# Gathers of the unit two ahead spread over the first product, all seven row splits beside the last three tiles of the second

## The chip, the cores and the metric

The kernel runs on one core of one Trainium2 chip. The metric is the device time of one execution in microseconds (us). TensorE (PE) multiplies, VectorE (DVE) and ScalarE (ACT) do the elementwise work, GpSimd (POOL) does some of it and issues the indirect DMAs (gathers and scatters by row number), SyncE (SP) issues plain DMAs and DMA transposes. Each engine, and each engine's queue of DMA issues, works strictly in the order of the program; engines wait for each other by semaphores.

## The reference

A block-sparse attention is followed by a top-2 mixture of experts. The part that matters here is the second:

```python
def _moe_ref(x, w_gate, w_noise, noise, w1, w2) -> np.ndarray:
    N, D = x.shape                      # 3072, 512
    E = w_gate.shape[1]                 # 8 experts, w1[e] 512x1024, w2[e] 1024x512
    ...
    top2 = np.argpartition(-noisy_logits, 2, axis=1)[:, :2]
    ...
    for e in range(E):
        for k in range(2):
            mask = top2[:, k] == e
            ...
            h = np.maximum(x[mask] @ w1[e], 0.0)
            out[mask] += top2_w[mask, k, None] * (h @ w2[e])
    return out.astype(np.float32)
```

## The kernel before, in words

The first half of the run is attention and routing and is not touched. The second half works through nine units, numbered u = 0 to 8: u = 0 and u = 1 share expert 0, and u = 2 to 8 are the experts 1 to 7 with 816 rows each, six chunks of 128 rows and one of 48. Every unit gathers its rows, splits them into a high and a low float16 half, turns them, multiplies by w1 (the first product), applies the rectifier, multiplies by w2 (the second product) and adds its weighted rows to the output by an indirect DMA.

From u = 3 on (`BLOCKS = 3`) the first product, `mm1_blocks`, uses seven block products in the place of eight. It runs in four sets i = 0 to 3. A set is seven products of six matmuls into PSUM banks named `ph`; ACT copies the first two banks to SBUF (lines L1026 and L1029, tile `area`), DVE adds and subtracts banks and copies (L1022), and `hidden` (L999 on ACT, L1000 on DVE) makes the high and low halves `hh`, `hl`. The fourth product of a set adds to the first bank, so PE cannot begin it until ACT has copied that bank. In the middle of each set one quarter of w2 is split: two ACT operations (L851, L852) and one subtraction on POOL (L853, tile `w2l`).

The second product, `mm2`, takes seven tiles k = 0 to 6, one for each chunk of rows, and each tile ends in `finish`: ACT scales the bank into one of three buffers `y` (L1104) and POOL scatters it with an add (L1109). Before tile k, `make_next(u + 1, k)` prepares the next unit: the splits of its w1 blocks (L880, L881), the sums of its row blocks and their splits into `tx` (L889 to L902), and the loads of its raw weights `wraw` on SP (L834), which rotate through six buffers. `row_split(1)`, the last of these splits, is needed by the fifth product of the next unit's first set.

Rows are fetched two units ahead. `meta` and `indices` are two small DVE operations (L909, L915), `gather` one indirect DMA on POOL for each chunk (L929) into the only row buffer `xg`; so a chunk can be gathered for the next unit only after the chunk of that number has been split. A split is one ACT copy (L948) and one DVE subtraction (L949) into one of five buffers `xs`, and one DMA transpose on SP (L953) turns it into `xt`, of which there are two, one for even and one for odd units. `xg`, `xs` and some other tiles lie in one large tile that the profile calls `kv`.

In the kernel before, this fetch is cut into pieces, by hand: chunks 0 to 3 of unit u + 2 are gathered before the last tile of unit u - 1, chunks 4 to 6 at sets 0 to 2 of unit u; chunks 0 to 2 are split ahead of set 0 of unit u (`halves`) and turned at tile 0; chunk 3 is split and turned at tile 0, and chunks 4, 5 and 6 at tiles 3, 4 and 5.

Of the kernel before, what the change touches and what calls it, by code (L numbers as in the profile page):

```python
# [747 lines left out]
class Experts:  # L748
# [188 lines left out]
                    self.tc.declare_no_dep(g.ins, s.ins, reason="other rows")  # L937
            ro.early.append(g)

    def row_halves(self, u, c):  # L940
        r = self.st["u", u]
        if "xt" not in r:
            pool, x = (self.xta, "a") if u % 2 == 0 else (self.xtb, "b")
            r["xt"] = pool.tile([P, self.KB, 2, 7 * P], F16, name="xt" + x)
        x = self.xg[:, c].rearrange("p (k c) -> p k c", c=P)
        xs = r["xs", c] = self.xs[0]
        self.xs = self.xs[1:] + self.xs[:1]
        self.nc.scalar.activation(xs[:, :, 0], x, AF.Copy)  # L948
        self.nc.vector.tensor_tensor(xs[:, :, 1], x, xs[:, :, 0], op=ALU.subtract)  # L949

    def turn_halves(self, u, c):
        r = self.st["u", u]
        self.nc.sync.dma_start_transpose(out=r["xt"][:, :, :, c * P:(c + 1) * P].rearrange("p k a r -> p (k a) r"),  # L953
                                         in_=r.pop(("xs", c)).rearrange("p k a c -> p (k a c)"))

    def xpose(self, u, c):
        self.row_halves(u, c)
        self.turn_halves(u, c)

    def chunks(self, u):  # L960

# [251 lines left out]
def kernel(ctx, tc, q, k, v, v_windows, sampled_blocks, w_gate, w_noise, noise, w1, w2, out):  # L1213
# [11 lines left out]
    ex = Experts(tc, router, w1, w2, out, x_dram, table)  # L1225
# [136 lines left out]
    nu = len(ex.units)  # L1362
# [31 lines left out]
            rest = third()  # L1394
            next(rest)

    def gathers(u, chunks):
        for i in chunks:
            ex.gather(u, i)

    def halves(u, chunks):
        for i in chunks:
            ex.row_halves(u, i)

    def fetch(u, chunks=None):
        ex.meta(u)
        ex.indices(u)
        gathers(u, range(ex.count(u)) if chunks is None else chunks)

    def make_next(u, k):  # L1410
        e = ex.units[u][1]
        if k == 0:
            if u + 1 < nu:
                for c in range(3):
                    ex.turn_halves(u + 1, c)
            for n in range(0 if u == BLOCKS else 2, 4):
                ex.weight_sum(e, 0, n)
            ex.weight_split(e, 0, 0)
            ex.load_piece(e, 4)
        elif k == 1:  # L1420
            ex.weight_split(e, 0, 1)
            ex.load_piece(e, 5)
        elif k == 2:
            ex.weight_split(e, 0, 2)
            ex.row_parts(u)
            ex.load_piece(e, 6)
        elif k == 3:
            ex.row_sums()
        elif k == 4:
            for n in range(4):  # L1430
                ex.weight_sum(e, 1, n)
            ex.weight_split(e, 1, 0)
        elif k == 5:
            ex.weight_split(e, 1, 1)
            ex.row_split(0)
            ex.load_piece(e, 7)
        else:
            ex.weight_split(e, 1, 2)
            ex.row_split(1)
        if u + 1 < nu and k in (0, 3, 4, 5):  # L1440
            ex.xpose(u + 1, {0: 3, 3: 4, 4: 5, 5: 6}[k])
        if u + 2 < nu and k == 6:
            fetch(u + 2, range(4))

    for u in range(nu):
        if u == 2:
# [5 lines left out]
        n = full + bool(left_)  # L1452
        nx = 1 < u < nu - 1
        if u >= BLOCKS:
# [5 lines left out]
            for i in range(ex.FB // 2):  # L1460
                if u + 2 < nu:
                    if i == 0:
                        halves(u + 2, range(3))
                    gathers(u + 2, ((4,), (5,), (6,), ())[i])
                ex.mm1_blocks(u, i, early)
                if nx:
                    for j in ((0, 1, 2), (3,), (), ())[i]:
# [1 line left out]
        else:  # L1469
            for f in range(ex.FB):  # L1470
# [13 lines left out]
                if u == 2:  # L1484
# [9 lines left out]
                            ex.load_piece(e + 1, i)  # L1494
                    if f == 5:
                        fetch(4)
                    if f == 7:
                        halves(4, range(3))
        for k, c in enumerate(ex.chunks(u)):
            if nx:  # L1500
                make_next(u + 1, k)
# [72 lines left out]
```

## Time and profile before

| what | us |
|---|---|
| median of three runs | 872.43 |
| lowest and highest of the three | 862.88, 872.71 |
| the profiled execution | 867.12 |
| its span | 865.1 |

The span is the time from the first to the last instruction on the core; the 2.0 us between it and the time of the profiled execution lie around it. All times in the rows below are counted from the start of the span. Units u = 3 to 8 begin their first products at 447.26, 518.17, 589.20, 660.50, 730.37 and 793.38 us.

### The profile page before, as it was taken

To read this page: it belongs to the slowest core of one execution; us is meant where nothing else is said; L and a number is where in the kernel's file an instruction comes from. 1 tells how busy PE (TensorE), PEld (TensorE's weight loads), DVE (VectorE), ACT (ScalarE), POOL (GpSimd) and SP (SyncE) were. 2 spreads that over 40 slices of the span, in tenths; PEclk is the share of its full clock that TensorE was granted. 3 is DMA by queue.
4 is the path that set the end of the run, shared out by engine and by line. 5 is a ranking of instruction groups with operands and counts; after the bars stand their busy time and mean duration, and the time that the engine had idled before them with its cause. 6 is when DMAs were issued, how large, how long until landed. Compare 5 with 4: busy or idle time off the path is not lost.

```text
span 865.1 us, 20964 instructions
## 1 busy us (share of the span) xinstructions
PE 778.4 (90%) x8505; PEld 461.6 (53%) x8505; DVE 551.7 (64%) x1086; ACT 417.6 (48%) x730; POOL 335.8 (39%) x525
## 2 busy tenths in 40 slices
PE   3899869988987799999988997997997999999995
PEld 1567657766666676565434443543543544544542
DVE  4676568767596566516776784784785686785620
ACT  2575544545662533525446554644645546635610
POOL 2566555622374200614544225235324332333232
PEclk9999898999997999999998998998999999999998
DMA  9988996881596985959993675367179267343013
GB/s 326 318 248 258 287 271 221 287 269 52 168 264 165 207 291 185 213 156 169 302 196 105 124 129 149 82 136 203 37 153 196 84 137 155 85 98 50 1 27 52
DMA packets 136249, 148.22 MB, mean 171 GB/s; under 512 B 65988, under 2 KB 101828, under 8 KB 136144
## 3 DMA queue, kind: packets, MB, share of 16 engines
q1 hardware_dynamic: 97200, 75.76, 32.0%
q0 software_dynamic: 16720, 45.77, 22.7%
q10 hardware_dynamic: 22224, 25.27, 10.1%
q8 instruction: 69, 1.13, 0.5%
q14 instruction: 36, 0.29, 0.1%
HBM read 105.87 MB, written 27.10 MB: 154 GB/s over the span
## 4 chain that ended last, share of the span: by engine, by line
PE 20%; issue 17%; DMA 9%; POOL 5%; ACT 2%; DVE 1%; POOLq 0%; ACTq 0%
PE ph L1018 13%; PE py L1062 7%; DMA out_dram<-y,mt 7%; POOL out_dram L1109 2%; DMA kv<-x_rows,gi 2%; POOL kv L929 1%; POOL w2l L853 1%; DVE area L1022 1%; ACT hh L999 1%; PE py L1073 1%; ACT w2h L852 0%; ACT wraw L851 0%; ACT area L1026 0%; ACT area L1029 0%; POOLq L1109 0%
## 5 line engine op out<-in xcount | busy, mean ns | idle before, releaser
L1109 POOL DMA_INDIRECT out_dram<-y,mt x56 | 86.6, 1546 | 243.2 <-ACT y L1104 188.9
L1062 PE MATMUL py<-w2h,hh 128*128 128x512 f16 x384 | 145.6, 379 | 0.0
L1062 PE MATMUL py<-w2h,hl 128*128 128x512 f16 x384 | 145.5, 379 | 0.0
L1062 PE MATMUL py<-w2l,hh 128*128 128x512 f16 x384 | 145.5, 379 | 0.0
L1062 PEld LDWEIGHTS <-hh 128*128 128x128 f16 x768 | 74.6, 98 | 90.1 <-issue 2.5
L317 ACT ACTIVATE t<-t 128x512 f32<-128x512 f32 (+1 forms) x120 | 63.1, 567 | 99.3 <-PE t L315 98.6
L1018 PEld LDWEIGHTS <-w1a 128*128 128x128 f16 x672 | 67.5, 100 | 77.7 <-issue 29.7
L1104 ACT ACTIVATE y<-py,r_tab 128x512 f32<-128x512 f32 (+1 forms) x55 | 37.7, 685 | 137.8 <-PE py L1062 90.8
L1018 PE MATMUL ph<-tx,w1a 128*128 128x408 f16 x384 | 101.5, 347 | 0.0
L214 POOL COPY kg<-kv 128x128 f32 x264 | 70.3, 311 | 51.0 <-issue 17.6
L853 POOL TENSOR_TENSOR w2l<-wraw,w2h 128x1024 f16<-128x1024 f32 x24 | 51.6, 2149 | 96.5 <-ACT w2h L852 96.5
L303 ACT ACTIVATE p<-s,nm 128x256 f32<-128x256 f32 x176 | 69.5, 480 | 25.6 <-DVE nm L264 24.0
L929 POOL DMA_INDIRECT kv<-x_rows,gi x56 | 60.9, 1088 | 46.5 <-DVE gi L915 23.9
L315 PE MATMUL t<-ident,p 128*128 128x128 f32 x448 | 70.5, 299 | 4.5 <-ACT p L303 2.2
L1000 DVE SCALAR_TENSOR_TENSOR hl<-ph,hh 128x408 f16<-128x408 f32 (+2 forms) x64 | 32.5, 531 | 59.9 <-ACT hh L999 59.9
L315 PEld LDWEIGHTS t<-ident,p 128*128 128x128 f32 x448 | 51.3, 149 | 36.4 <-issue 17.9
L1022 DVE TENSOR_TENSOR area<-ph,area 128x408 f32<-128x408 f32 x96 | 53.5, 578 | 21.5 <-PE ph L1018 14.3
L999 ACT ACTIVATE hh<-area 128x408 f16<-128x408 f32 (+1 forms) x48 | 33.0, 713 | 70.8 <-DVE area L1022 70.8
L1018 PE MATMUL ph<-tx,w1b 128*128 128x408 f16 x192 | 66.2, 345 | 0.0
L243 PE MATMUL s<-kg,q 64*32 64x256 f32 x1408 | 56.5, 404 | 9.2 <-issue 4.8
L949 DVE TENSOR_TENSOR kv<-kv 128x512 f16<-128x512 f32 x56 | 38.3, 689 | 40.9 <-ACT kv L948 40.8
L264 DVE TENSOR_REDUCE nm<-s 128x4 f32<-128x1024 f32 (+1 forms) x48 | 54.2, 1129 | 14.2 <-PE s L243 13.2
(202 smaller groups left out, 1439.6 us busy)
## 6 DMA issues: line engine op xcount, KB each, us to landing
wraw<-in_moe_w_dram SPq DMA_DIRECT2D x64, 512.0 KB, 5.6
vb<-in_v_windows_dram ACTq DMA_DIRECT2D x24, 390.0 KB, 5.5
vb<-in_v_windows_dram ACTq DMA_DIRECT2D x16, 520.0 KB, 6.1
kv<-in_v_dram SPq DMA_DIRECT2D x4, 1560.0 KB, 15.6
q<-in_q_dram SPq DMA_DIRECT2D x12, 512.0 KB, 6.3
kv<-in_k_dram SPq DMA_DIRECT2D x8, 768.0 KB, 9.5
out_dram<-zero ACTq DMA_DIRECT2D x8, 768.0 KB, 4.8
x_rows<-xr SPq DMA_DIRECT2D x19, 256.0 KB, 3.9
```

What stands on the lines that cost most here:

```text
L214: nc.gpsimd.tensor_copy(KG[:, j, :, 32 * s:32 * s + 32], KT[:, :, bass.ds(offs[3 * j + s], 32)])
L243: mm = lambda out, l, r, pos: nc.tensor.matmul(out, l, r, start=True, stop=True, tile_position=pos)
L264: red = lambda out, x: nc.vector.tensor_reduce(out, x, axis=AX.X, op=ALU.max, negate=True)
L303: self.nc.scalar.activation(p[:, 256 * u:256 * u + 256], S[:, a, 256 * r:256 * r + 256], AF.Exp, bias=nb[:, u:u + 1], scale=1.0 if k else ...
L315: self.nc.tensor.transpose(T[i][:, c:c + P], p[:, i * w + c:i * w + c + P], self.ident)
L317: self.nc.scalar.activation(t[:, i * w:(i + 1) * w], T[i][:, 0:w], AF.Copy)
L853: self.nc.gpsimd.tensor_tensor(lo, t, hi, op=ALU.subtract)
L929: g = nc.gpsimd.indirect_dma_start(out=self.xg[0:m, c], out_offset=None, in_=self.x_dram[0:nr], in_offset=bass.IndirectOffsetOnAxis(ap=r[" ...
L1018: nc.tensor.matmul(bank[:, 0:HC], self.wop[part][:, w, kb, fs], b(kb, a), start=start and n == 0, stop=n == 5, skip_group_check=True)
L1022: add = lambda e, out, p, q: e.tensor_tensor(out, p, q, op=ALU.add)
L1062: nc.tensor.matmul(py, h[:, f, o], w[x][:, f, :], start=i == 0, stop=i == last)
L1109: s = nc.gpsimd.indirect_dma_start(out=self.out, out_offset=bass.IndirectOffsetOnAxis(ap=r["mt"][0:m, c:c + 1], axis=0), in_=y[0:m], in_of ...
```

## The change

The gathers of unit u + 2 now all stand in the first product of unit u, two ahead of each of the sets 0, 1 and 2 and one ahead of set 3, with `meta` and `indices` ahead of set 0. All seven splits, each with its transpose, stand in the second product of unit u: two before tile 4, two before tile 5, three before tile 6, each time behind the work on the next unit's weights and row sums. Nothing is added or taken out; `row_halves` and `turn_halves` become one function again.

```diff
-    def row_halves(self, u, c):
+    def xpose(self, u, c):
...
-        xs = r["xs", c] = self.xs[0]
+        xs = self.xs[0]
         self.xs = self.xs[1:] + self.xs[:1]
         self.nc.scalar.activation(xs[:, :, 0], x, AF.Copy)
         self.nc.vector.tensor_tensor(xs[:, :, 1], x, xs[:, :, 0], op=ALU.subtract)
-
-    def turn_halves(self, u, c):
-        r = self.st["u", u]
         self.nc.sync.dma_start_transpose(out=r["xt"][:, :, :, c * P:(c + 1) * P].rearrange("p k a r -> p (k a) r"),
...
     def make_next(u, k):
         e = ex.units[u][1]
         if k == 0:
-            if u + 1 < nu:
-                for c in range(3):
-                    ex.turn_halves(u + 1, c)
...
-        if u + 1 < nu and k in (0, 3, 4, 5):
-            ex.xpose(u + 1, {0: 3, 3: 4, 4: 5, 5: 6}[k])
-        if u + 2 < nu and k == 6:
-            fetch(u + 2, range(4))
+        if u + 1 < nu and k > 3:
+            for c in range(ex.count(u + 1))[2 * k - 8:2 * k - 6 if k < 6 else None]:
+                ex.xpose(u + 1, c)
...
             for i in range(ex.FB // 2):
                 if u + 2 < nu:
                     if i == 0:
-                        halves(u + 2, range(3))
-                    gathers(u + 2, ((4,), (5,), (6,), ())[i])
+                        ex.meta(u + 2)
+                        ex.indices(u + 2)
+                    for c in range(2 * i, min(2 * i + 2, n)):
+                        ex.gather(u + 2, c)
                 ex.mm1_blocks(u, i, early)
...
                     if f == 5:
                         fetch(4)
-                    if f == 7:
-                        halves(4, range(3))
```

How the order of instructions moves is shown at two engines, at the border between two units (the same at the borders ahead of u = 3, 4, 5 and 6). First ACT, before: the last two tiles of a unit's second product, then set 0 of the next unit. L880 and L901 are the next unit's splits, L1104 the tile's scaling into `y`, L948 the row splits, L1026 the copy of the first bank.

```order
L1104 ACTIVATE y<-py,r_tab 128x512
L880 ACTIVATE w1a<-wraw 128x4x256
L901 ACTIVATE tx<-area 128x4x408
L948 ACTIVATE kv_89<-kv_89 128x4x128
L1104 ACTIVATE y<-py,r_tab 128x512
L880 ACTIVATE w1a<-area 128x6x256
L901 ACTIVATE tx<-area 128x4x408
L1104 ACTIVATE y<-py,r_tab 128x512
L948 ACTIVATE kv_89<-kv_89 128x4x128 x3
L1026 ACTIVATE area<-ph 128x408
```

The same place of ACT in the changed kernel (its lines have other numbers: L1097 is the scaling into `y`, L1019 the copy of the first bank):

```order
L1097 ACTIVATE y<-py,r_tab 128x512
L880 ACTIVATE w1a<-wraw 128x4x256
L901 ACTIVATE tx<-area 128x4x408
L948 ACTIVATE kv_89<-kv_89 128x4x128 x2
L1097 ACTIVATE y<-py,r_tab 128x512
L880 ACTIVATE w1a<-area 128x6x256
L901 ACTIVATE tx<-area 128x4x408
L948 ACTIVATE kv_89<-kv_89 128x4x128 x3
L1097 ACTIVATE y<-py,r_tab 128x512
L1019 ACTIVATE area<-ph 128x408
```

The three splits have moved from behind the last tile's scaling to ahead of it, and they are now those of chunks 4 to 6, gathered a product earlier. Next POOL, before, from the scatters of one unit's second product to its next:

```order
L1109 DMA out_dram<-y,mt 3072x512 x6
L929 DMA kv_89<-x_rows,gi 128x512 x4
L1109 DMA out_dram<-y,mt 3072x512
L929 DMA kv_89<-x_rows,gi 128x512
L853 TENSOR_TENSOR w2l<-wraw,w2h 128x1024
L929 DMA kv_89<-x_rows,gi 128x512
L853 TENSOR_TENSOR w2l<-wraw,w2h 128x1024
L929 DMA kv_89<-x_rows,gi 48x512
L853 TENSOR_TENSOR w2l<-wraw,w2h 128x1024 x2
```

The same place of POOL in the changed kernel (L1102 is the scatter):

```order
L1102 DMA out_dram<-y,mt 3072x512 x7
L929 DMA kv_89<-x_rows,gi 128x512 x2
L853 TENSOR_TENSOR w2l<-wraw,w2h 128x1024
L929 DMA kv_89<-x_rows,gi 128x512 x2
L853 TENSOR_TENSOR w2l<-wraw,w2h 128x1024
L929 DMA kv_89<-x_rows,gi 128x512 x2
L853 TENSOR_TENSOR w2l<-wraw,w2h 128x1024
L929 DMA kv_89<-x_rows,gi 48x512
L853 TENSOR_TENSOR w2l<-wraw,w2h 128x1024
```

The four gathers that stood ahead of the seventh scatter now stand behind it, and the first `w2l` of the unit has two gathers ahead of it and the seventh scatter ahead of those.

## Rows read from the trace of the kernel before

**Rows 1.** Waits of PE from 440 us on: us in total, times, longest.

```profile
PE ph L1018 <- ACT area L1026: 22.3, 4, 6.0
```

**Rows 2.** Timeline of PE (start, us, what): first matmuls of units 3, 5, 7, 8.

```profile
447.26 0.51 PE L1018 MATMUL ph<-xtb,w1a 128*128 128x408 f16 x2
...
589.20 0.51 PE L1018 MATMUL ph<-xtb,w1a 128*128 128x408 f16 x2
...
730.37 0.51 PE L1018 MATMUL ph<-xtb,w1a 128*128 128x408 f16 x2
...
793.38 0.51 PE L1018 MATMUL ph<-xta,w1a 128*128 128x408 f16 x2
```

**Rows 3.** Timeline of PE in set 0 of unit 5; brackets: idle before, releaser.

```profile
592.13 0.34 PE L1018 MATMUL ph<-tx,w1b 128*128 128x408 f16 x1
597.85 0.84 PE L1018 MATMUL ph<-xtb,w1a 128*128 128x408 f16 x2 [5.39 <-ACT area L1026]
...
603.85 0.34 PE L1018 MATMUL ph<-xtb,w1a 128*128 128x408 f16 x1
```

**Rows 4.** Stretches: busy us and instructions by engine, granted clock, DMA share, GB/s.

```profile
598.00:603.00 5.00, 5.00 (x16) 2.22 (x15) 1.29 (x3) 2.60 (x4) 3.51 (x3) 0.50 0.48 93
...
731.00:760.00 29.00, 29.00 (x169) 16.31 (x167) 18.52 (x32) 17.49 (x27) 10.10 (x5) 1.00 0.37 97
```

**Rows 5.** Timeline of ACT at the border from unit 4 to 5.

```profile
586.22 1.55 ACT L901 ACTIVATE tx<-area 128x1632 f16<-128x1632 f32 x1
589.45 0.69 ACT L1104 ACTIVATE y<-py,r_tab 128x512 f32<-128x512 f32 x1 [1.67 <-issue]
594.62 0.63 ACT L948 ACTIVATE kv<-kv 128x512 f16<-128x512 f32 x1 [4.49 <-DMA kv<-x_rows,gi]
...
597.31 0.49 ACT L1026 ACTIVATE area<-ph 128x408 f32<-128x408 f32 x1
```

**Rows 6.** Timeline of POOL at the same border.

```profile
590.44 1.07 POOL L929 DMA_INDIRECT kv<-x_rows,gi  x1 [3.66 <-DVE gi L915]
...
595.77 1.70 POOL L1109 DMA_INDIRECT out_dram<-y,mt  x1 [0.30 <-issue]
```

**Rows 7.** Timeline of DVE from tile 4 of unit 4 to that border.

```profile
579.17 0.68 DVE L949 TENSOR_TENSOR kv<-kv 128x512 f16<-128x512 f32 x1
...
588.03 1.85 DVE L902 TENSOR_TENSOR tx<-area,tx 128x1632 f16<-128x1632 f32 x1
...
590.00 0.17 DVE L915 TENSOR_SCALAR gi<-mt 128x7 int32<-128x7 int32 x1
595.28 0.69 DVE L949 TENSOR_TENSOR kv<-kv 128x512 f16<-128x512 f32 x1 [5.11 <-ACT kv L948]
```

**Rows 8.** Stretch of tiles 4 to 6 of unit 4; columns: PE, PEld, DVE, ACT, POOL.

```profile
573.70:589.20 15.50, 15.50 (x74) 6.98 (x73) 12.62 (x14) 9.27 (x10) 4.68 (x3) 1.00 0.73 134
```

**Rows 9.** DMA from issue to landing: transposes to xta, 440 to 735 us.

```profile
DMA to landing us min/median/max: 3.1/4.1/6.2
```

**Rows 10.** The same of the raw weights' loads, 440 to 800 us.

```profile
DMA to landing us min/median/max: 3.3/5.7/8.7
```

**Rows 11.** Timeline of POOL at the border from unit 6 to 7.

```profile
726.40 1.55 POOL L1109 DMA_INDIRECT out_dram<-y,mt  x1 [3.68 <-ACT y L1104]
735.33 1.55 POOL L1109 DMA_INDIRECT out_dram<-y,mt  x1 [7.38 <-ACT w2h L852]
736.34 2.71 POOL L853 TENSOR_TENSOR w2l<-wraw,w2h 128x1024 f16<-128x1024 f32 x1
743.32 2.13 POOL L853 TENSOR_TENSOR w2l<-wraw,w2h 128x1024 f16<-128x1024 f32 x1 [4.27 <-ACT w2h L852]
```

**Rows 12.** Timeline of DVE in sets 0 and 2 of unit 7.

```profile
738.39 1.11 DVE L1022 TENSOR_TENSOR area<-area 128x408 f32<-128x408 f32 x1
...
748.22 0.68 DVE L863 TENSOR_TENSOR area<-wraw 128x512 f32<-128x512 f32 x1
748.82 0.57 DVE L1022 TENSOR_TENSOR area<-ph,area 128x408 f32<-128x408 f32 x1
```

More of the change, by code (lines that the diff above doesn't have):

```diff
@@ L949, in row_halves @@
         self.nc.vector.tensor_tensor(xs[:, :, 1], x, xs[:, :, 0], op=ALU.subtract)
-    def turn_halves(self, u, c):
-        r = self.st["u", u]
         self.nc.sync.dma_start_transpose(out=r["xt"][:, :, :, c * P:(c + 1) * P].rearrange("p k a r -> p (k a) r"),
[L954 to L958, printed above, removed]
+                                         in_=xs.rearrange("p k a c -> p (k a c)"))
     def chunks(self, u):
@@ L1395, in turn, with fetch @@
             next(rest)
[L1397 to L1405, printed above, removed]
+    def fetch(u):
         ex.meta(u)
         ex.indices(u)
-        gathers(u, range(ex.count(u)) if chunks is None else chunks)
+        for i in range(ex.count(u)):
+            ex.gather(u, i)
     def make_next(u, k):
```

## The prediction

> **What bounds the kernel now.** I read the busy table by stretches first: from 447 us on, PE is the engine that is hardly ever idle, so a gain must come from PE's idle time or from a clock below full. The list of PE's waits in this stretch then has one line only: 22.3 us in four waits, on ACT's copy of the first bank [rows 1]. Four is the number of units that fetch rows for a unit two ahead while they run their first product (u = 3 to 6). The timeline of PE gives the price whole. Units 3 to 6 take 730.37 - 447.26 = 283.11 us, 70.8 each; unit 7 makes the same products and the next unit's weights but fetches nothing, and takes 793.38 - 730.37 = 63.01 [rows 2]. So 7.8 us a unit is lost.
>
> The timeline inside set 0 of unit 5 shows the two parts of it. After 18 matmuls PE stands for 5.39 us [rows 3], and then the granted clock is 0.50, the 1.2 GHz level: 16 matmuls in 5 us against 169 in 29 us at the full level [rows 4]. The slow stretch runs from 597.85 to 603.85 [rows 3]; at 29/169 = 0.17 us a matmul instead of 5/16 = 0.31 it costs some 2.5 us. 5.4 + 2.5 is the 7.8 within the error of the reading.
>
> The chain behind the idle time, read from ACT, POOL and DVE at that border: DVE finishes the last row-block split at 588.03 + 1.85 = 589.88 and only then makes the indices (590.00) [rows 7]; POOL starts the first gather at 590.44 [rows 6]; its rows arrive and ACT's first row split starts at 594.62 after 4.49 us of waiting for that DMA; two more splits follow, and the bank's copy comes at 597.31 [rows 5]. The bank itself was full 1.0 us after 589.20 (six matmuls of 0.17). PE waits for a gather that has nothing to do with the product it is in.
>
> **The change part by part.** B is the moment at which a unit's first product begins (589.20 in the rows, 730.37 for unit 7).
>
> Taken away: the three row splits ahead of set 0. They were the only work on ACT there that waited for a gather. In the changed order ACT's next instruction after the tile's scaling is the bank's copy. What is late next is PE itself: at the border into unit 7 ACT has just this order, and PE's timeline has no idle time through it and the granted clock is 1.00 [rows 4]. So I take unit 7's 63.01 us for units 3 to 6: 4 x 63.01 = 252.04, a gain of 283.11 - 252.04 = 31.07 us.
>
> Added to tiles 4 to 6: seven splits where three stood, four more of 0.63 us on ACT and 0.69 on DVE [rows 5, 7]. That stretch lasts 15.5 us of PE time; ACT is busy 9.27 and DVE 12.62 in it [rows 8]. With the change ACT has 9.3 + 4 x 0.63 = 11.8, DVE 12.6 + 4 x 0.69 = 15.4: DVE is full to the brim. What matters is who stands behind what. `row_split(1)` stands ahead of the last three splits, and the four earlier ones fill time in which DVE waited, so it ends where it did, at about B + 0.7; were the added 2.8 us all in front of it, B + 3.5. PE needs it for its fifth group of six, B + 24 x 0.17 = B + 4.1. The last three splits run to B + 0.7 + 3 x 0.69 = B + 2.8, the indices to B + 3.1. The first DVE addition of set 0 reads the third bank, ready at B + 18 x 0.17 = B + 3.1, and PE waits for that addition only at the seventh group, B + 36 x 0.17 = B + 6.2. Cover 2.5 us, cost nothing; with all of the 2.8 in front 0.3 us a border, 1.2 in all.
>
> On ACT the three late copies follow the split that ends at 586.22 + 1.55 = B - 1.4 and end at B + 0.5; the last tile's scaling, which began at 589.45 = B + 0.25 [rows 5], is 0.2 us later. The bank's copy is then possible at B + 1.2, and PE wants the bank again at B + 18 x 0.17 = B + 3.1. Cost nothing.
>
> The transposes: three now go out at about B + 1.5 to B + 4, and the next loads of raw weights, which stood ahead of them in SP's queue, come behind, at about B + 4. Their landing takes 5.7 us, 8.7 at most [rows 10], so B + 13 at the latest; the first reader of such a load is the weight sum of set 2, in unit 7 at 748.22 = B + 17.9 [rows 12]. Cover 5 us, cost nothing. The turned rows are read a whole unit later. Earlier loads for w2 lose three transposes ahead of them at tile 0.
>
> The gathers: seven at 1.07 us of POOL [rows 6], all in the first product, read at tile 4 some 40 us later; their landing is hidden. But they stand ahead of `w2l`, and the first two now also behind the seventh scatter, which waits for the landing of the sixth. In unit 7 the sixth was issued at 726.40 = B - 4.0 and the seventh at 735.33 = B + 5.0 [rows 11]. With 1.55 for the scatter and two gathers of 1.07 with some 0.3 between them, `w2l` starts at about B + 9.2 at the latest and ends at B + 11.3; if the sixth lands early, two or three us sooner. Behind it is the load of raw piece 2, which takes its buffer: landed at B + 17 (5.7) or B + 20 (8.7). Its reader is the weight sum just named; behind that, on DVE, is the third set's first addition (748.82 [rows 12]), for which PE waits from the seventh group of set 2 on, B + 84 x 0.17 + 6.2 = B + 20.6, and sum and addition take 1.2 us, so the load has until B + 19.4. Cost nothing at the usual landing, 0.6 us a border with both at their worst; below nothing is excluded, since PE has no idle time in unit 7 to give.
>
> At this place a rule speaks against the change. In unit 7 the first `w2l` took 2.71 us where the next one took 2.13 [rows 11], and the DVE subtraction of two SBUF operands that fell into it 1.11 us [rows 12]: each lost about half a microsecond. The Trainium skill ("SBUF — State Buffer", section "Who interferes with whom") says that a DVE instruction with two SBUF inputs and a GpSimd instruction that reads SBUF share a read interface, and that the second to start is blocked until the first ends. The trace agrees that the two hurt each other; no row here shows a block for the whole length. By the row the sum stays as it is, since unit 7's 63.01 holds that loss. By the rule the loss could be the whole 2.13 in set 0 of four units, 1.6 more each, 6.4 in all if nothing covered it, which would make 843 of the sum below.
>
> The sum, against the profiled execution: 867.1 - 31.1 = 836.0, and 1 us for the borders above (0 to 3.6 by the bounds) makes 837. The median of the three runs lies 5.3 above the profiled execution and the lowest 4.2 below; if that spread lies outside the four gaps, the changed kernel's runs spread from 833 to 842. I take **838**.
>
> **The rivals.** First, part of the gain comes back at `w2l`: the seventh scatter is later than in unit 7, because the gathers and transposes share the DMA engines with it, the load of piece 2 comes after B + 19.4, DVE waits for it in order, and PE stands in set 2. For it: at B the DMA share was high, and the reserve is 2 us only at the usual landing. Against: piece 2's load is the only transfer in that hurry. At 1 us a border it is 842, at 3 us with a slow stretch of 2.5 behind it 838 + 4 x 5.5 = 860; I put it at 846.
>
> Second, slower: the five `xs` buffers. The sixth split takes the buffer of the first, the seventh that of the second, 8 us after those were handed to the transposes; before, the reuse was a product apart. ACT waits in order, and behind it stand the last scaling and the bank's copy: the same gap as now, with another name. By the rows the second transpose goes out at about 579.17 + 0.68 + 1.2 = B - 8.1 and lands by B - 1.9 at the worst (6.2 [rows 9]); ACT asks at B - 0.3. It decides from a landing of 7.8 us on, and to lose more than the 7.8 us of today the landing must take 14 to 16: then 867 + 4 x 2 = 875. Nothing in the rows comes near.
>
> Third, the change does not take the gap away, because ACT is held at the same place by something the wait on the gather hides today: 867 to 872. Against it stands unit 7. Fourth, the shared interface of the paragraph above, 843.
>
> **How the numbers follow.** The forecast (gaps gone, 832 to 843) has a chance of 0.77; the return at `w2l` 0.12; the shared interface 0.04; the gap that stays 0.04; the ring of five, slower, 0.03. The likeliest gives 838. For the range I go below to 828, since a pace set by PE leaves little under 832, and above to 854, which takes in most of the first rival. A change of 2% is 17.4 us, about what a measurement of this kernel can tell from none: faster means under 855. The forecast, the shared interface and most of the first rival are faster, 0.89; same 0.08; slower 0.03.
>
> **What the changed profile would show.** Right: PE's waits have no line on ACT's first bank copy, units 3 to 7 are 63 us each, the granted clock is 1.00 from 447 us to the last unit; ACT's row splits stand in tiles 4 to 6 and wait for no DMA; POOL's first `w2l` of a unit starts between B + 6 and B + 9. Wrong: idle time of PE in set 2 with DVE's weight sum waiting for a load (first rival); ACT's sixth or seventh split waiting for a transpose (second); idle time in set 0 under another name (third). The prediction fails as a whole if the units stay at 70 us, or if dense work without these pauses lowers the granted clock, which the 63 us of unit 7 and what follows them do not show.

## The result, and the profile after

The changed kernel takes 841.72 us (median; 836.16 to 846.43) where the kernel before, run beside it (the three executions of the table ahead and a fourth), takes 867.96 (862.88 to 872.71): a ratio of 0.970, 95% interval 0.960 to 0.979. It is faster, and 3.7 us above the 838 that were predicted. The profiled execution took 842.40, its span is 840.6; 837 was the sum for it.

The list of PE's waits from 440 us on still has one line, under the same two names as in [rows 1], but with 5.7 us where 22.3 stood, and with five waits where there were four (in this kernel L1011 is the first product's matmul, L1015 DVE's adding and subtracting, L1019 the first bank's copy, L992 the rectifier):

```profile
PE ph L1011 <- ACT area L1019: 5.7, 5, 1.9
```

The timeline of PE shows the first matmuls of units 3, 5, 7 and 8 (as [rows 2]) and, between them, where the wait of unit 5 lies:

```profile
448.11 0.51 PE L1011 MATMUL ph<-xtb,w1a 128*128 128x408 f16 x2
...
576.20 0.51 PE L1011 MATMUL ph<-xtb,w1a 128*128 128x408 f16 x2
...
588.66 0.51 PE L1011 MATMUL ph<-xtb,w1a 128*128 128x408 f16 x2 [1.95 <-ACT area L1019]
...
705.46 0.51 PE L1011 MATMUL ph<-xtb,w1a 128*128 128x408 f16 x2
...
768.94 0.51 PE L1011 MATMUL ph<-xta,w1a 128*128 128x408 f16 x2
```

Units 3 to 6 now take 705.46 - 448.11 = 257.35 us (283.11 before, 252.04 predicted), unit 7 63.48 (63.01 before). From the first matmul of unit 3 to that of unit 8 it is 320.83 us, against 793.38 - 447.26 = 346.12; this stretch is the measure for the experiments below. The gap of set 0 is gone: the wait at 588.66 = B + 12.46 (B is 576.20 here) is in set 1, at its fourth product. The stretches of tiles 4 to 6 of unit 4 and of unit 3 (columns: PE, PEld, DVE, ACT, POOL, granted clock, DMA share, GB/s) answer to [rows 4] and [rows 8]:

```profile
560.70:576.20 15.50, 15.50 (x73) 7.01 (x72) 13.22 (x15) 11.72 (x15) 4.64 (x3) 1.00 0.78 137
...
447.00:510.00 63.00, 61.31 (x329) 30.83 (x328) 49.32 (x67) 34.70 (x50) 26.95 (x18) 1.00 0.64 146
```

The granted clock is 1.00, the 2.4 GHz level, in unit 3 in spite of its wait of 1.69 us. ACT is busy 11.72 us in the three tiles; 11.8 was predicted. ACT's timeline at the border from unit 4 to 5 (as [rows 5]):

```profile
574.69 1.66 ACT L948 ACTIVATE kv<-kv 128x512 f16<-128x512 f32 x3
576.40 0.69 ACT L1097 ACTIVATE y<-py,r_tab 128x512 f32<-128x512 f32 x1
577.44 0.51 ACT L1019 ACTIVATE area<-ph 128x408 f32<-128x408 f32 x1 [0.35 <-PE ph L1011]
...
587.33 0.88 ACT L992 ACTIVATE hh<-area 128x816 f16<-128x816 f32 x1 [2.45 <-DVE area L1015]
588.12 0.49 ACT L1019 ACTIVATE area<-ph 128x408 f32<-128x408 f32 x1
```

The splits wait for no DMA, and the first bank is copied at B + 1.24. The new wait is in the last two rows: the copy of set 1's first bank stands in ACT's queue behind a rectifier (`hh`, the high half of set 0), and that one waits 2.45 us for DVE. DVE's timeline at the same place (as [rows 7]):

```profile
575.04 1.85 DVE L902 TENSOR_TENSOR tx<-area,tx 128x1632 f16<-128x1632 f32 x1
576.81 1.89 DVE L949 TENSOR_TENSOR kv<-kv 128x512 f16<-128x512 f32 x3
...
578.81 0.17 DVE L915 TENSOR_SCALAR gi<-mt 128x7 int32<-128x7 int32 x1
579.58 0.58 DVE L1015 TENSOR_TENSOR area<-ph,area 128x408 f32<-128x408 f32 x1 [0.60 <-PE ph L1011]
...
584.22 3.07 DVE L1015 TENSOR_TENSOR area<-area 128x408 f32<-128x408 f32 x1
```

The last row is the subtraction `c22`, whose two operands lie in SBUF. Here it lasts 3.07 us; in unit 8, 0.57:

```profile
776.96 0.57 DVE L1015 TENSOR_TENSOR area<-area 128x408 f32<-128x408 f32 x1
```

POOL's timeline (as [rows 6]) shows what runs beside it:

```profile
580.44 1.54 POOL L1102 DMA_INDIRECT out_dram<-y,mt  x1 [6.66 <-ACT wraw L851]
582.28 1.08 POOL L929 DMA_INDIRECT kv<-x_rows,gi  x1 [0.30 <-DVE hl L993]
583.67 1.02 POOL L929 DMA_INDIRECT kv<-x_rows,gi  x1 [0.31 <-issue]
584.71 2.13 POOL L853 TENSOR_TENSOR w2l<-wraw,w2h 128x1024 f16<-128x1024 f32 x1
```

`w2l` ends at 586.84, `c22` at 587.29, 0.45 us behind it. The same 0.45 stands between the two ends in all five units:

| unit | `w2l` starts, ends | `c22` lasts (from B + 8.02) | PE then waits |
|---|---|---|---|
| 3 | B + 8.26, 10.39 | 2.82 | 1.69 |
| 4 | B + 6.90, 9.04 | 1.47 | 0.34 |
| 5 | B + 8.51, 10.64 | 3.07 | 1.95 |
| 6 | B + 7.81, 9.94 | 2.37 | 1.25 |
| 7 | B + 6.44, 9.15 | 1.58 | 0.45 |

PE's wait is, in each row and to 0.01 us, what `c22` lasts beyond 0.57 less 0.55 us of reserve; put otherwise, the end of `w2l` less B + 8.69. Over the 62.87 us that a unit without such a wait takes (e2) the five units lose 6.5 us, each 0.16 more than its wait in the list. The transfers that the prediction had to cover stay inside the times that it allowed (7.8 and 8.7 us), though the transposes' median has risen from 4.1 to 5.3: transposes to `xta` (from 440 to 735 us, as [rows 9]), then raw weights (440 to 800 us, as [rows 10]), each from issue to landing:

```profile
DMA to landing us min/median/max: 3.5/5.3/6.9
```

```profile
DMA to landing us min/median/max: 3.4/4.9/8.1
```

### The profile page after: what moved, and what is told of

The parts are those of the page before. It is cut to its first block, busy times and chain, and to the rows that moved or that the text cites. A ratio compares the mean times of both kernels' runs of the same rounds, so it can differ in the third digit from the quotient of the medians.

```text
span 840.6 us, 20979 instructions
## 1 busy us (share of the span) xinstructions
PE 766.2 (91%) x8505; PEld 455.6 (54%) x8505; DVE 557.9 (66%) x1086; ACT 417.0 (50%) x730; POOL 340.6 (41%) x525
## 4 chain that ended last, share of the span: by engine, by line
PE 69%; issue 9%; DVE 8%; DMA 6%; POOL 3%; ACT 2%; SPq 1%; POOLq 0%; DVEq 0%; ACTq 0%
PE py L1055 23%; PE ph L1011 16%; PE ph L983 8%; PE po L330 6%; PE t L315 5%; PE s L243 5%; DVE area L1015 2%; DMA q<-in_q_dram 2%; PE py L1066 2%; PE pe L572 2%; DMA kv<-in_k_dram 2%; PE po L736 1%; DVE nm L264 1%; POOL out_dram L1102 1%; DMA kv<-x_rows,gi 1%
## 5 line engine op out<-in xcount | busy, mean ns | idle before, releaser
L1102 POOL DMA_INDIRECT out_dram<-y,mt x56 | 86.7, 1548 | 265.3 <-ACT y L1097 184.0
L1097 ACT ACTIVATE y<-py,r_tab 128x512 f32<-128x512 f32 (+1 forms) x55 | 37.7, 685 | 133.8 <-PE py L1055 116.7
L1011 PE MATMUL ph<-tx,w1a 128*128 128x408 f16 x384 | 97.7, 336 | 0.0
L1011 PEld LDWEIGHTS <-w1a 128*128 128x128 f16 x672 | 65.7, 98 | 57.2 <-issue 6.9
L929 POOL DMA_INDIRECT kv<-x_rows,gi x56 | 62.7, 1120 | 30.9 <-issue 21.6
L992 ACT ACTIVATE hh<-area 128x408 f16<-128x408 f32 (+1 forms) x48 | 33.2, 713 | 70.7 <-DVE area L1015 70.7
L1011 PE MATMUL ph<-tx,w1b 128*128 128x408 f16 x192 | 64.5, 336 | 0.0
L1015 DVE TENSOR_TENSOR area<-ph,area 128x408 f32<-128x408 f32 x96 | 53.5, 578 | 13.8 <-PE ph L1011 9.2
L1055 PEld LDWEIGHTS <-hl 128*128 128x128 f16 x384 | 37.5, 98 | 45.7 <-DVE hl L993 0.5
```

What stands on the lines that cost most here:

```text
L929: g = nc.gpsimd.indirect_dma_start(out=self.xg[0:m, c], out_offset=None, in_=self.x_dram[0:nr], in_offset=bass.IndirectOffsetOnAxis(ap=r[" ...
L1011: nc.tensor.matmul(bank[:, 0:HC], self.wop[part][:, w, kb, fs], b(kb, a), start=start and n == 0, stop=n == 5, skip_group_check=True)
L1015: add = lambda e, out, p, q: e.tensor_tensor(out, p, q, op=ALU.add)
L1055: nc.tensor.matmul(py, h[:, f, o], w[x][:, f, :], start=i == 0, stop=i == last)
L1102: s = nc.gpsimd.indirect_dma_start(out=self.out, out_offset=bass.IndirectOffsetOnAxis(ap=r["mt"][0:m, c:c + 1], axis=0), in_=y[0:m], in_of ...
```

## The experiments

Theory 1: what the changed kernel lost against the forecast is `c22` held by POOL's `w2l`, passed on to PE by ACT's queue order. Its rivals: DVE is simply too full at the borders; the load behind `w2l` comes late (the first rival of the prediction); the waits are chance landings of DMAs. Up to unit 2 the code is the same in all kernels, but unit 3 begins anywhere from 447.3 to 457.5 us from one profiled execution to the next (at 448.1 and 452.6 in the two of the changed kernel), so single profiled executions are compared by the stretch from unit 3 to unit 8. Line numbers differ by a few between the kernels (L1019 is DVE's addition in e2 and ACT's copy in e6): go by the engine and the names.

| kernel | stretch, us | PE waits on ph in it, us | median time (before on the same chip) |
|---|---|---|---|
| before | 346.12 | 22.3 | 867.96 |
| changed | 320.83 | 5.7 | 841.72 (867.96) |
| e1 gathers behind `w2l` | 317.11 | 2.4 | 843.52 (876.72) |
| e2 `w2l` writes only | 314.35 | 0 | 840.97, one execution (876.72) |
| e3 seven gathers ahead | 334.78 | 14.6 | 863.6, one (876.72) |
| e4 only the splits moved | 317.14 | 0 | 846.8 (876.72) |
| e5 changed, again | 319.91 | 4.9 | 843.81 (868.31) |
| e6 bank copies first | 314.75 | 0 | 836.15 (868.31) |
| e7 ring of three | 329.33 | 12.0 | 856.41, one (868.31) |
| e8 `w2l` twice | 319.35 | 4.2 | 842.38, one (868.31) |
| e9 `w2l` in four pieces | 319.24 | 4.2 | 845.79, one (878.36, one) |
| e10 a split a tile | 316.63 | 1.8 | 848.18, one (878.36, one) |

**e1: each set's gathers behind its `w2l`.**

```diff
-                    for c in range(2 * i, min(2 * i + 2, n)):
-                        ex.gather(u + 2, c)
                 ex.mm1_blocks(u, i, early)
+                if u + 2 < nu:
+                    for c in range(2 * i, min(2 * i + 2, n)):
+                        ex.gather(u + 2, c)
```

> The changed kernel with each set's gathers issued on POOL behind that set's w2 subtraction instead of ahead of it. Theory 1 (shared SBUF interface: POOL's w2 subtraction, pushed late by the seventh scatter and two gathers, falls onto DVE's subtraction of two SBUF operands at the end of set 0, ACT's high half waits for it, and ACT's copy of set 1's first bank stands behind that): the w2 subtraction of set 0 starts 2.7 us sooner, at about B + 5.8, and ends before or just into the DVE operation. That operation falls from 1.5 to 3.1 us in units 3 to 6 to between 0.57 and 1.1, PE's waits on the bank copy from 5.7 us to under 2, and the units take 63.0 to 63.5 us. Theory 2 (DVE is simply full with seven splits beside the last three tiles, and is late in set 0 whatever POOL does): 5.7 us of PE waits stay and the units take 63.4 to 65.0.

Ratio to before 0.963 (0.958 to 0.968). Units 4, 5 and 6 take 62.87 us each, and `c22` lasts 0.57, 0.61 and 0.78 in them. POOL and DVE in unit 5 (B is 583.70):

```profile
588.17 1.54 POOL L1102 DMA_INDIRECT out_dram<-y,mt  x1 [6.89 <-PE ph L1011]
589.16 2.71 POOL L853 TENSOR_TENSOR w2l<-wraw,w2h 128x1024 f16<-128x1024 f32 x1
```

```profile
591.72 0.61 DVE L1015 TENSOR_TENSOR area<-area 128x408 f32<-128x408 f32 x1
```

`w2l` ends at 591.87 and `c22` at 592.33, 0.46 behind: they still meet, but only at the tail. Unit 3 went otherwise: a scatter there kept POOL for 8.13 us, `w2l` began at B + 10.43, the next ones after it, and set 1's subtraction was held instead:

```profile
471.11 3.08 DVE L1015 TENSOR_TENSOR area<-area 128x408 f32<-128x408 f32 x1
```

PE then waited 1.96 us in set 2 (the rest of the 2.4 is 0.48 in unit 7, which has no gathers to move). So it is the two operations' meeting that costs, in whichever set it falls. The time cannot be set against the changed kernel's, which ran on another chip.

**e2: the first quarter's `w2l` only writes.** Two fills of `lo` stand for the subtraction, so this quarter of the low half of w2 is zero.

```diff
-            self.nc.gpsimd.tensor_tensor(lo, t, hi, op=ALU.subtract)
+            if i == 4 and e >= 2:
+                for _ in range(2):
+                    self.nc.gpsimd.memset(lo, 0.0)
+            else:
+                self.nc.gpsimd.tensor_tensor(lo, t, hi, op=ALU.subtract)
```

> The changed kernel, but the first quarter of w2's low half is not computed: two POOL fills that only write take the place of the subtraction in set 0 (that quarter of the low half is zero). Gathers, scatter and splits stand where they stood. Theory 1: a POOL instruction that reads no SBUF does not hold DVE up, so the DVE subtraction in set 0 takes 0.57 us in every unit and PE has no wait on the bank copy (0 to 0.5 us in all), with DVE just as full as before. Theory 2: 5.7 us of waits stay. If the fills hold DVE up as well, it is POOL's writing and not its reading that is shared.

All five units take 62.87 us, with no wait of PE. POOL, then DVE, in unit 4:

```profile
522.32 1.98 POOL L855 MEMSET w2l<- 128x1024 f16 x2
```

```profile
523.49 0.57 DVE L1019 TENSOR_TENSOR area<-area 128x408 f32<-128x408 f32 x1
```

`c22` lies wholly inside the fills and lasts its 0.57 us. DVE has the same work as in the changed kernel, so fullness of DVE is out; it is POOL's reading beside it that holds `c22`.

**e3: all seven gathers ahead of set 0's `w2l`.**

```diff
-                    for c in range(2 * i, min(2 * i + 2, n)):
+                    for c in range(n) if i == 0 else ():
                         ex.gather(u + 2, c)
```

> The changed kernel with all seven gathers ahead of set 0's w2 subtraction. Five more gathers of about 1.35 us push it to about B + 15, and the load of raw piece 2 behind it lands at B + 23 or later, where the first rival of the prediction says that it has until B + 19.4. Theory of that rival: DVE's first weight sum waits 3 to 6 us for that load in set 2, PE stands in set 2 or at set 3's fourth product, 3 to 6 us a border, 12 to 24 in all with a stretch at half clock behind the longer ones, span 850 to 865; the DVE subtraction in set 0 is 0.57 us, since the w2 subtraction is not yet there. If that load is in no hurry: span 834 to 842.

The stretch is 334.78 us: a late `w2l` costs. But no wait for the load behind it is seen: DVE's waits from 440 us on have no entry on a load of raw weights. PE's waits in that time, and then POOL and DVE in unit 3 (B is 455.25):

```profile
PE ph L1011 <- DVE area L1015: 8.3, 2, 4.1
PE ph L1011 <- ACT area L1019: 6.3, 3, 3.6
```

```profile
471.93 6.29 POOL L853 TENSOR_TENSOR w2l<-wraw,w2h 128x1024 f16<-128x1024 f32 x3
```

```profile
472.04 7.06 DVE L993 SCALAR_TENSOR_TENSOR hl<-area,hh 128x816 f16<-128x816 f32 x1 [0.25 <-issue]
```

Three `w2l` that had piled up run back to back, and the making of `hl`, again with two SBUF operands (1.01 us elsewhere), is held through all three; PE waits 4.1 us, and the granted clock is 0.70 in the 5.8 us behind that. My expectation had the right side and, in the load, the wrong cause; but the weight sum stands behind `hl` on DVE and begins at 479.02, so a load that landed before then would not show here.

**e4: before, with only the three splits moved**, one each ahead of sets 1, 2 and 3; the gathers stay as they were.

```diff
                 if u + 2 < nu:
-                    if i == 0:
-                        halves(u + 2, range(3))
+                    if i > 0:
+                        halves(u + 2, (i - 1,))
                     gathers(u + 2, ((4,), (5,), (6,), ())[i])
```

> The kernel before with one thing moved: the splits of chunks 0, 1 and 2 stand ahead of sets 1, 2 and 3 of the first product (one each) instead of all ahead of set 0. Gathers, transposes and everything else as before. If the gap came from ACT waiting for a gather ahead of set 0's bank copy and from nothing else, it is gone at all four borders, PE's idle time there falls from 22.3 us to under 6 (what a w2 subtraction behind five gathers and a scatter may cost DVE), the granted clock is 1.00, and the span is 834 to 842. If the gathers themselves had to be moved, PE waits as long as before at set 1, and the span stays over 855.

Ratio to before 0.966 (0.961 to 0.971); units 3 to 6 take 63.54 to 63.58, where they took 70.8 (the 0.7 over 62.87 are four steps too short for PE's list, in unit 4: 0.12, 0.27 and 0.13 us at the fourth products of sets 1 to 3, on ACT's bank copy, which has a row split right ahead of it now; and 0.17 us at the seventh product of set 1). The gap was the splits on ACT ahead of the bank's copy and nothing else; the gathers need not have moved. Four gathers and the scatter ahead of it put `w2l` at B + 9.6 here, behind `c22`; it meets the making of `hl`'s high half instead. POOL, then DVE, in unit 4:

```profile
528.54 2.14 POOL L853 TENSOR_TENSOR w2l<-wraw,w2h 128x1024 f16<-128x1024 f32 x1
```

```profile
528.49 3.06 DVE L1000 SCALAR_TENSOR_TENSOR hl<-area,hh 128x816 f16<-128x816 f32 x1 [0.25 <-ACT hh L999]
```

It lasts 3.06 in the place of 1.01, and PE's list has no wait: this half of `hl` is read by the second product alone, and the bank copies on ACT stand behind nothing that reads it. What reaches PE is the step of 0.17 us at the seventh product: that one waits for a DVE addition, which stands behind the held `hl`. The span, 844.4, is above the 834 to 842 that I expected.

**e5: the changed kernel again**, on the chip of e6 to e8.

> The changed kernel unchanged, on the same chip as the three beside it, so that they can be compared with it. Theory 1 (the loss left in the changed kernel is a DVE subtraction that stands still while POOL's first w2l of a unit runs): from the first matmul of unit 3 to that of unit 8 some 320 us, PE waits on ACT's copy of the first bank in set 1 of up to five units, each 0.55 us shorter than what the subtraction lasts beyond 0.57. Theory 2 (those waits come from how the DMAs happened to land in one profiled execution): the waits are elsewhere or gone, and the stretch is 314 to 316.

Ratio to before 0.970 (0.966 to 0.975), stretch 319.91. PE waits 0.79, 0.34, 1.70 and 2.09 us in units 3 to 6, where `c22` lasts 1.92, 1.47, 2.83 and 3.22: each wait is 0.56 less than the excess over 0.57. In unit 7 it lasts 0.95, and PE does not wait. What varies from one execution to the next is when the seventh scatter can go (B + 2.6 to B + 4.8), and `w2l` with it; the rule holds. In unit 3 the weight sum waits for its load, as the first rival said, until B + 19.91:

```profile
472.54 0.69 DVE L863 TENSOR_TENSOR area<-wraw 128x512 f32<-128x512 f32 x1 [1.17 <-DMA wraw<-in_moe_w_dram]
```

That unit takes 63.82 us, 0.95 over 62.87, which is its wait in set 1 and the 0.16: the load costs PE nothing.

**e6: the two bank copies ahead of the former set's high half on ACT.**

```diff
         nc.scalar.activation(s7, V[:, 0:HC], AF.Copy)
+        for f in getattr(self, "late", None) or ():
+            self.hidden(f, 0, 2 * HC, self.both)
+        self.late = None
         early()
...
-        self.hidden(i + F, 0, 2 * HC, self.both)
+        self.late = [i + F] if i < F - 1 else self.hidden(i + F, 0, 2 * HC, self.both)
```

> The changed kernel, but in sets 1 to 3 the rectifier of the former set's high half (which reads the sums that DVE is late with) stands behind the set's two bank copies on ACT, not ahead of them. The DVE subtraction still collides with w2l and still takes 1.5 to 3 us. Theory 1 (what PE waits for is ACT's queue order: the copy stands behind a rectifier that waits for the blocked subtraction): PE's waits on the first bank copy are gone, units 3 to 7 are 62.9 to 63.3 each, the stretch from unit 3 to unit 8 is 314.4 to 316, 5 us under the changed kernel beside it. Rival (the blocked DVE itself is what costs, since its next bank addition comes late too): the wait comes back under the name of a DVE addition and the stretch stays at 318 to 321.

836.15 us (829.97 to 838.42), ratio to before 0.961 (0.955 to 0.967); the changed kernel beside it took 843.81 (841.11 to 846.39), and no execution of the one reaches the other's. The stretch is 314.75, 5.2 us shorter; the rest of the difference between the two profiled executions lies, but for 0.4 us, ahead of unit 3, where the edit changes nothing. DVE, then ACT, in unit 5 (B is 573.70; L1019 and L1022 are the two bank copies):

```profile
581.72 3.19 DVE L1015 TENSOR_TENSOR area<-area 128x408 f32<-128x408 f32 x1
```

```profile
582.28 0.49 ACT L1019 ACTIVATE area<-ph 128x408 f32<-128x408 f32 x1
583.22 0.51 ACT L1022 ACTIVATE area<-ph 128x408 f32<-128x408 f32 x1 [0.44 <-PE ph L1011]
584.94 0.88 ACT L992 ACTIVATE hh<-area 128x816 f16<-128x816 f32 x1 [1.21 <-DVE area L1015]
```

`c22` is held as long as ever, the rectifier waits as it did, and the copy is no longer behind it: PE's list has no wait. The rival's way is there and small: two products of this unit, which takes 63.26 us, begin 0.25 and 0.15 late, on DVE's additions. The second link of theory 1, ACT's queue order, is shown, and this version beats both kernels.

**e7: three `xs` buffers in the place of five** (the second rival, made sharper).

```diff
-                    for o in range(7 * self.D, 12 * self.D, self.D)]
+                    for o in range(7 * self.D, 10 * self.D, self.D)]
```

> The changed kernel with three xs buffers in the place of five, so that the fourth to seventh split of a unit each take a buffer whose transpose went out shortly before. The second rival of the prediction says that such reuse holds ACT, and behind it the scaling of the last tile and the bank's copy: PE waits on the bank copy in set 0 come back, at least 4 us in each of units 4 to 8, and the stretch from unit 3 to unit 8 is over 335. Theory 1 of the prediction (transposes land in 3 to 6 us and the splits stand far enough apart) says that five buffers have reserve; with three it expects ACT to wait for transposes by some 2 to 4 us at the border, and PE to lose 0 to 3 us a unit: the stretch 320 to 335.

ACT's waits from 430 to 800 us now name the transposes:

```profile
ACT kv L948 <- DMA xta<-kv: 10.6, 6, 3.2
ACT kv L948 <- DMA xtb<-kv: 7.8, 4, 3.1
```

PE waits on the first bank copy in set 0 again, 1.70, 1.46, 0.60, 2.52 and 3.09 us in units 3 to 7. The rival's mechanism exists and with three buffers costs 9 us in the stretch; the rival's own price for five, over 7.8 us a unit, is not reached even here.

**e8: the first quarter's `w2l` done twice.**

```diff
-            self.nc.gpsimd.tensor_tensor(lo, t, hi, op=ALU.subtract)
+            for _ in range(2 if i == 4 else 1):
+                self.nc.gpsimd.tensor_tensor(lo, t, hi, op=ALU.subtract)
```

> The changed kernel, but POOL does the low half of the first quarter of w2 twice, one right behind the other (the result is the same). The stretch in which POOL reads SBUF is 4.3 us where it was 2.1. Theory 1a (DVE's two-operand subtraction stays blocked as long as POOL goes on reading): the subtraction lasts 3.6 to 5.3 us, PE's wait in set 1 is some 2.2 us longer in each of units 3 to 7, 16 us in sum where it was 5.7, and the stretch is 330 or more. Theory 1b (the block ends with the POOL instruction, DVE goes next, and POOL's second one waits): the subtraction lasts as before, the second w2l takes 2.7 to 3 us, PE's waits stay at 5 to 7 us in sum, the stretch 320 to 323. If neither matters (no block), nothing changes against the changed kernel beyond 0.5 us.

PE's waits do not grow (4.2 us in the stretch, and 0.6 in unit 8). POOL, then DVE, in unit 5:

```profile
583.85 4.58 POOL L854 TENSOR_TENSOR w2l<-wraw,w2h 128x1024 f16<-128x1024 f32 x2
```

```profile
583.82 2.63 DVE L1016 TENSOR_TENSOR area<-area 128x408 f32<-128x408 f32 x1
586.37 3.42 DVE L994 SCALAR_TENSOR_TENSOR hl<-area,hh 128x408 f16<-128x408 f32 x2
```

`c22` ends at 586.45, in the middle of the two; POOL's pair lasts 4.58 where 2 x 2.13 = 4.26 would do, and the first of DVE's next two two-operand operations is held by the second. Here DVE got in between, as 1b said (with 2.7 to 3 us for the second `w2l`, which takes 2.36).

**e9: the first quarter's `w2l` in four pieces**, which write different columns.

```diff
-            self.nc.gpsimd.tensor_tensor(lo, t, hi, op=ALU.subtract)
+            for q in ([slice(j * 128, j * 128 + 128) for j in range(4)] if i == 4 else [slice(None)]):
+                self.nc.gpsimd.tensor_tensor(lo[:, :, q], t[:, :, q], hi[:, :, q], op=ALU.subtract)
```

> The changed kernel, but POOL's low half of the first quarter of w2 is made by four instructions of a quarter of the columns each, in the place of one; they write different columns and do not wait for each other. In the run with all gathers ahead, two and three w2l back to back held a DVE operation to the end of the last; in the run with w2l done twice (the second writes what the first wrote) DVE got in between. Theory A (instructions of POOL that follow without a wait hold DVE as one): DVE's subtraction ends with the last of the four and lasts 1.5 to 3.3 us as in the changed kernel, PE's waits are 4.5 to 7 us in sum, the stretch from unit 3 to unit 8 is 319 to 323. Theory B (the block ends with each instruction, some 0.55 us): the subtraction lasts at most 1.2 us, PE waits at most 0.1 us a unit, the stretch 314.4 to 315.5.

Neither theory's numbers. POOL, then DVE, in unit 3 (B is 452.70):

```profile
461.25 3.95 POOL L854 TENSOR_TENSOR w2l<-wraw,w2h 128x256 f16<-128x256 f32 x4
```

```profile
460.72 0.95 DVE L1016 TENSOR_TENSOR area<-area 128x408 f32<-128x408 f32 x1
...
467.97 2.33 DVE L1016 TENSOR_TENSOR area<-area 128x408 f32<-128x408 f32 x1
```

Set 0's `c22` escapes with 0.57 to 0.95 us in four units (1.64 in unit 4), as theory B has it; but the four pieces take 2.9 to 3.95 us between DVE's operations, the second quarter's `w2l` is later for it and holds set 1's subtraction, and PE waits in set 2 (1.20, 1.10, 1.44 us). The loss moved on by one set.

**e10: a row split ahead of each tile**, not all at the last three.

```diff
-        if u + 1 < nu and k > 3:
-            for c in range(ex.count(u + 1))[2 * k - 8:2 * k - 6 if k < 6 else None]:
-                ex.xpose(u + 1, c)
+        if u + 1 < nu and k < ex.count(u + 1):
+            ex.xpose(u + 1, k)
```

> The changed kernel, but the seven row splits stand one ahead of each of the seven tiles of the second product, not at the last three. The gathers that they wait for were issued in the first product, 10 us or more earlier. If the dense last three tiles cost something (DVE full there, the transposes late, the loads of raw weights behind them), the borders between units are better for it and the stretch from unit 3 to unit 8 falls below the changed kernel's 320 by more than the change in the w2l collisions. Theory 1 (the dense stretch is covered; only w2l against the DVE subtraction is left): PE's waits keep the name of the first bank copy in set 1, each 0.55 us under the excess of the subtraction over 0.57, and nothing else changes; the stretch is 314.4 plus the sum of those waits, within 0.5.

The stretch is 316.63, and three units take 62.87. That is theory 1's sum, 314.4 and the two waits of 1.8 us in all, within 0.5; what changed is how `w2l` meets `c22`. The crowded tiles may have a part in that: the seventh scatter waits for the landing of the sixth. In unit 5 of the changed kernel the sixth went out at 572.23 and the seventh at 580.44, 8.2 us later, with five transposes issued between 571.65 and 581.52; the sixth landed 7.5 us after its issue. Here, ahead of unit 5 (B is 585.55):

```profile
581.58 1.54 POOL L1102 DMA_INDIRECT out_dram<-y,mt  x1 [3.37 <-ACT y L1097]
587.38 1.54 POOL L1102 DMA_INDIRECT out_dram<-y,mt  x1 [4.26 <-ACT area L1019]
...
591.66 2.13 POOL L853 TENSOR_TENSOR w2l<-wraw,w2h 128x1024 f16<-128x1024 f32 x1
```

The distance is 5.8 us, so `w2l` starts at B + 6.11 and only its last bit meets `c22` (0.69 us). In unit 3, though, a scatter kept POOL 7.04 us, as in e1, and the loss (1.33 us) came in set 3. That the transposes lengthen the landing is argued and not shown: in unit 4 the two scatters stand 6.6 us apart in the changed kernel and 6.7 here, and before the change, ahead of unit 7, they stood 8.9 apart [rows 11] with one transpose and the raw loads issued beside them. One execution does not tell how much of the 3 to 4 us against the changed kernel is the placing.

## Why the prediction was right, and where it was not

*The bound and the gap: right.* PE sets the pace; the gap was the splits' wait on ACT, as e4 shows, and the slow clock behind it went with it. The base of a unit, 63.01, was right to 0.14: units without a wait take 62.87, and the 0.14 is a step of PE in unit 7 at the fourth product of set 1, on ACT's copy, where the waits lie now. Of the signs of being right two came only in part: PE's list kept its line, in another set, and units 3 to 7 are 63.4 to 65.0 us.

*Tiles 4 to 6: right but for DVE's load.* DVE is busy 13.22 us there, not 15.4: the last three splits, which the prediction itself puts behind B, do not fall into that stretch. `row_split` was to end at B + 0.7 and ends at 576.89 = B + 0.69; the splits at B + 2.5 (predicted 2.8), the indices at B + 2.8 (3.1), the bank copy at B + 1.24 (1.2). The first addition of set 0 waits for PE, not the other way round. The transposes and loads land within their cover; no split and no weight sum waits for a DMA in this execution. The step did not ask whether the crowd of transposes delays the seventh scatter, which e10 leaves open.

*The gathers and `w2l`: this step failed.* `w2l` began at B + 6.4 to 8.5, within what was worked out (B + 9.2 at the latest), but "cost nothing", and with it the 1 us for the borders, was wrong: it cost 5.7 us of PE's waits, 6.5 us of time. Against the sum of 837, units 3 to 6 give 257.35 - 252.04 = 5.3 more, less the 1 us allowed; unit 7 gives 0.5, and what lies outside the stretch 0.6: 5.4, which is 842.40 - 837. I had asked who waits for what comes behind `w2l` on POOL and its buffer, and not what runs beside it.

*The paragraph on the rule misread the rows.* I wrote that each of the two lost half a microsecond and that no row showed a block for the whole length. The record of `w2l` in [rows 11] starts at 736.34, inside the scatter's record, which runs to 735.33 + 1.55 = 736.88; from there it lasts 2.17, so it lost nothing. It ends at 739.05, and the subtraction of [rows 12] at 739.50: 0.45 us behind, as in the five units after. The rows did show the block; only its tail lay over the subtraction there. The Trainium skill ("SBUF — State Buffer", section "Who interferes with whom") has it that a DVE operation with two SBUF inputs contends with a GpSimd operation that reads SBUF, not with one that only writes it. The runs agree: 3.07 us beside `w2l`, 0.57 beside the fills of e2.

*The rivals.* The fourth, given 0.04 and 843, is what happened on top of the forecast: 5.2 us in the four units where it had 6.4. I had counted it as the rival of a rule and not as a term of the sum, which it should have been. The first, given 0.12, is there in its wait and not in its price: in e2, e5, e9 and e10 a weight sum waits 0.2 to 1.2 us for a load in set 2, and PE loses at most 0.2 us by it; where `w2l` is late (e3), it is the same block that costs. The second exists (e7) and needs fewer buffers than there are. The third fell. The time lies in the range because the gain of 31 was sized rightly and what came back was small. That it was small is in part luck: neither the 0.55 us of reserve nor the moment at which the seventh scatter goes stood in the sum, and with a later `w2l` (e3) 14.6 us of waits came back.

## What to carry to other kernels

When an operation of POOL that reads SBUF moves, look for the two-operand DVE operations that it will now run beside, price them as held until it ends (here 0.45 us past its end for one of 0.57 us), and then follow the held result through the queue of whoever reads it. In these runs a wait of DVE reached PE only through what stood behind it in a queue: putting the two bank copies ahead of the rectifier (e6) took back the whole 5 us though the block stayed. Compare the ends of two records that overlap, not only their lengths, before saying who held whom.

## What the runs showed of the hardware that was not expected

The start of a record does not tell who came first: in unit 5 after, `c22` starts 0.49 us ahead of `w2l` and would have ended 0.08 behind its start, and is held to its end all the same. In unit 6 of e5 it starts 0.63 us ahead and would have ended before the start of `w2l`, and is held too. DVE, then POOL:

```profile
652.57 3.22 DVE L1015 TENSOR_TENSOR area<-area 128x408 f32<-128x408 f32 x1
```

```profile
653.20 2.14 POOL L853 TENSOR_TENSOR w2l<-wraw,w2h 128x1024 f16<-128x1024 f32 x1
```

In unit 3 of e10 DVE starts 0.77 us ahead, with the making of `hl`, and goes through in its usual time, while `w2l` is 0.11 us longer:

```profile
474.31 1.01 DVE L993 SCALAR_TENSOR_TENSOR hl<-area,hh 128x816 f16<-128x816 f32 x1 [0.25 <-ACT hh L992]
```

```profile
475.08 2.24 POOL L853 TENSOR_TENSOR w2l<-wraw,w2h 128x1024 f16<-128x1024 f32 x1
```

So by these records the one that starts second is not always the one that is held, as the prediction had the rule. What fits these records is a `w2l` that takes hold of what the two share more than 0.63 and less than 0.77 us ahead of its record's start; that is argued from these few cases and not tested.

POOL operations back to back let DVE in between in e8 (two on the same tile) and mostly in e9 (four short ones), and did not in e3: there three kept `hl` for 7.06 us, and in unit 5 two (604.73 to 608.93) kept a `c22` to 609.38. What decides is open.

The clock did not fall behind each wait. From the windows behind two waits in set 0 of e7, the first of 2.52 us, the second of 3.09 us:

```profile
654.20:664.00 9.80, 9.14 (x53) 5.08 (x53) 6.40 (x10) 6.33 (x10) 8.43 (x6) 1.00 0.95 245
...
721.14:726.00 4.86, 4.86 (x20) 2.37 (x20) 1.20 (x3) 2.75 (x4) 3.49 (x2) 0.68 0.79 122
```

It stayed at 1.00 behind the first and behind all of the changed kernel's (1.95 at most), and was at the 1.2 GHz level for a part of the second stretch. So no slow stretch came on top of the changed kernel's waits, as one did on top of the gaps before.

A scatter's issue held POOL for 8.13 us (e1) and 7.04 us (e10) at the border into unit 3, where it is 1.55 to 2.3 in the other runs; its cause was not tried.
